# Linformer attention and a squared-ReLU FFN on one core: first stages by head pairs, and pauses on GpSimd between the first load issues

## Chip, cores, metric

One NeuronCore of a Trainium2 chip. The metric is the device time of one execution in microseconds. A "span" is the time from the first to the last instruction of a profiled execution; here it is 1.7 to 2.2 us shorter than the device time.

## The reference

```python
def _attn_ref(q, k, v, E, F):            # q, k, v: (8, 8, 1024, 64), E, F: (64, 1024)
    k_proj = np.einsum('ks,bhsd->bhkd', E, k)
    v_proj = np.einsum('ks,bhsd->bhkd', F, v)
    scores = q @ k_proj^T / sqrt(64); attn = softmax(scores)       # shortened
    return attn @ v_proj
# then x = (8192, 512) and the FFN: relu(x @ w_in)**2 @ w_out, w_in (512, 2048), w_out (2048, 512)
```

## The kernel before

A batch has 8 heads of 1024 rows. The kernel has long been tuned: while the FFN of one batch runs, the attention of the next is fitted between its matmuls. Only batch 0 has nothing to hide behind. Its first half of rows is done in `first_stages`, and the FFN of that half follows at once. All inputs except `E` and `F` come in through GpSimd's queue, which casts fp32 to bf16 on the way. The loads are issued in the order in which they are needed:

```python
    for s in (slice(0, 4), slice(4, 8)):
        load_heads(K_first, k, s)                # two pieces of K, batch 0
    ident = const_pool.tile([P, P], BF16, name="ident")
    make_identity(nc, ident[:])
    load_q_half(0, slice(0, H))                  # the first half of Q's rows
    for s in (slice(0, 4), slice(4, 6), slice(6, 8)):
        load_heads(V_first, v, s)                # three pieces of V
    # ... then w_in in pieces, the second half of Q, w_out; later K, V, Q of batch 1
```

```python
        def first_stages(self):
            # filler(n): n matmuls of 512 columns whose result nobody reads
            filler(2); self.project_k(0); filler(1); self.transpose_k(0)
            self.project_k(1); filler(2); self.transpose_k(1); filler(1)     # (joined lines)
            for g in range(2):
                self.half_transpose_q(0, g, ffn_psum)
            for g in range(2):
                self.half_scores(0, g)
                self.half_exponentials(g)
            heads = [slice(0, 4), slice(4, 6), slice(6, 8)]
            self.project_v(heads[0])
            self.copy_v(heads[0])
            self.half_sums(0, apart=True)
            self.half_sums(1)
            self.half_reciprocals(0)
            self.half_reciprocals(1)
            self.half_values(0)
            for s in heads[1:]:
                self.project_v(s)
                self.copy_v(s)
            self.half_values(1)
            for g in range(2):
                for e in range(2):
                    self.half_normalize(0, g, e)         # writes xT, what the FFN reads
```

The FFN of batch 0 opens with 16 matmuls of 512 columns: four column blocks of `xT`, each against four blocks of `w_in`. At step 33 of the FFN, K and V of batch 1 are projected (`project`, into the tile `ps_kv`). That is the first use of batch 1's loads.

The softmax here doesn't subtract the row's maximum and nothing guards it: scores larger than these inputs give would overflow.

## Time and profile before

| | before |
|---|---|
| time, median of 3 runs (range) | 484.47 us (483.62 to 485.47) |
| span of the profiled run | 482.4 us |
| TensorE busy, share of the span | 97% |
| first FFN matmul starts | 21.05 us |
| V of batch 1 has landed | 53.27 us |
| first matmul on V of batch 1 | 53.32 us |

A landing, here and below, is the last of the 16 DMA engines' completion marks of one load, read from the trace's record. Lines of the page (busy us, share of the span, instructions):

```profile
span 482.4 us, 8423 instructions
...
PE 470.3 (97%) x3630; PEld 292.6 (61%) x3630; DVE 314.1 (65%) x382; ACT 261.5 (54%) x413; POOL 34.7 (7%) x48
...
q0 software_dynamic: 30624, 29.36, 39.4%
...
HBM read 59.24 MB, written 16.78 MB: 158 GB/s over the span
```

TensorE (PE) is all but full, so the kernel as a whole is bound by its matmuls. GpSimd's queue (q0) wrote 29.36 MB for 59.24 MB read: the cast halves the bytes, and a rate of 204 GB/s in the trace stands for 408 GB/s of reads.

The view by stretches, 4 to 12 us: first the stretch, then each engine's busy time, last what the loads wrote in GB/s.

```profile
4.00:6.00 2.00, 0.70 (x8) 0.57 (x8) 0.97 (x2) 0.00 (x0) 2.00 (x4) 1.00 1.10 175
6.00:8.00 2.00, 0.51 (x8) 0.51 (x8) 0.14 (x1) 1.04 (x1) 2.00 (x3) 1.00 1.08 145
8.00:10.00 2.00, 2.00 (x11) 0.96 (x10) 0.00 (x0) 0.59 (x1) 0.71 (x2) 1.00 1.20 191
10.00:12.00 2.00, 1.68 (x10) 0.77 (x8) 0.64 (x2) 0.00 (x0) 0.10 (x1) 1.00 1.38 197
```

From 10 us on the rate stays at 197 to 209 GB/s until 40 us. From 4 to 8 us it is lower, and in that time GpSimd issues loads without a gap.

The timeline before, cut (start, us, engine, line, operation, out<-in, count; in brackets the idle time ahead of it and what ended it):

```profile
3.00 0.90 POOL L97 DMA_DIRECT2D Q_sb<-in_q_dram  x1
...
4.21 2.42 POOL L93 DMA_DIRECT2D V_sb<-in_v_dram  x3
...
6.62 1.40 POOL L124 DMA_DIRECT2D w_in<-in_moe_w_in_dram  x2
...
9.11 1.92 PE L262 MATMUL ps_k<-K_sb,ET 128*64 128x256 bf16 x8
...
12.00 1.06 PE L262 MATMUL ps_k<-K_sb,ET 128*64 128x256 bf16 x8
...
19.43 0.48 PEld L284 LDWEIGHTS <-FT 128*64 128x64 bf16 x16 [0.21 <-DMA V_sb<-in_v_dram]
...
20.11 0.29 DVE L288 CAST vp<-ps_v 128x128 bf16<-128x128 f32 x1 [0.39 <-PE ps_v L284]
...
20.32 2.47 DVE L351 TENSOR_TENSOR xT<-ps_att,rs 128x512 bf16<-128x512 f32 x4
...
21.05 6.40 PE L459 MATMUL ps_h<-xT,w_in 128*128 128x512 bf16 x28 [0.19 <-DVE xT L351]
```

V's last piece lands at 19.39 us; its projection, a copy and one normalization lie between that and the first FFN matmul, 1.67 us in all.

The same view at 53 us, K and V of batch 1:

```profile
53.03 0.40 PE L180 MATMUL ps_kv<-K_sb,ET 128*64 128x512 bf16 x1
53.32 0.38 PE L181 MATMUL ps_kv<-V_sb,FT 128*64 128x512 bf16 x1
```

### The profile page before, as it was taken

The numbers are of one execution on the slowest core, as the hardware profiler recorded it, in microseconds if no ns is written. First come the engines' busy times: TensorE is split into PE (matmuls) and PEld (weight loads), VectorE is DVE, ScalarE is ACT, GpSimd is POOL, SyncE is SP. The second block draws the span as 40 slices with busy tenths as digits, with TensorE's granted clock in tenths as the row PEclk, the third lists the DMA queues.
The fourth block names the chain that finished last, engine by engine and source line by source line (L and its number), as shares of the span: only waits on it lengthen the run. The fifth ranks groups of instructions, "written<-read, shape, count | busy, mean of one in ns | idle before, by whom it ended". The sixth has DMA issues, their size and how long they took to land.

```text
span 482.4 us, 8423 instructions
## 1 busy us (share of the span) xinstructions
PE 470.3 (97%) x3630; PEld 292.6 (61%) x3630; DVE 314.1 (65%) x382; ACT 261.5 (54%) x413; POOL 34.7 (7%) x48
## 2 busy tenths in 40 slices
PE   4899999999999999999999999999999999999997
PEld 2544676475574746657475665747557474666656
DVE  1478955554958559493776848667494855948383
ACT  2387544758427564466635667176662756545351
POOL 6540020020020001000010000100000000000000
PEclk9999999999999999999999999999999999999999
DMA  9999989579989086941859147690702102020202
GB/s 155 203 204 207 168 181 200 137 120 229 180 128 229 12 175 88 180 94 50 153 86 227 22 115 131 91 200 1 165 11 75 25 1 88 1 88 0 88 1 87
DMA packets 72789, 55.46 MB, mean 115 GB/s; under 512 B 33968, under 2 KB 64944, under 8 KB 72752
## 3 DMA queue, kind: packets, MB, share of 16 engines
q0 software_dynamic: 30624, 29.36, 39.4%
q1 hardware_dynamic: 42128, 25.56, 21.1%
q8 instruction: 28, 0.46, 0.4%
q14 instruction: 9, 0.07, 0.0%
HBM read 59.24 MB, written 16.78 MB: 158 GB/s over the span
## 4 chain that ended last, share of the span: by engine, by line
PE 92%; DVE 3%; DMA 3%; ACT 1%; POOL 1%; issue 0%; POOLq 0%
PE ps_h L459 44%; PE ps_y L479 23%; PE ps_z L479 11%; PE ps_x L479 6%; DMA V_sb<-in_v_dram 3%; PE ps_kv L180 2%; PE ps_att L221 2%; PE ps_att L206 2%; DVE hsq L521 1%; DVE s L473 1%; PE ps_v L284 0%; DVE xT L246 0%; DVE xT L351 0%; PE ps_kv L181 0%; ACT h_relu L513 0%; POOL K_sb L93 0%
## 5 line engine op out<-in xcount | busy, mean ns | idle before, releaser
L459 PE MATMUL ps_h<-xT,w_in 128*128 128x512 bf16 x1024 | 224.8, 379 | 0.2 <-DVE xT L351 0.2
L521 DVE TENSOR_TENSOR hsq<-h_relu 128x1024 bf16<-128x1024 f32 x123 | 149.9, 1222 | 75.0 <-ACT h_relu L513 74.2
L513 ACT ACTIVATE h_relu<-ps_h 128x512 f32<-128x512 f32 x255 | 149.4, 597 | 63.4 <-PE ps_h L459 63.0
L459 PEld LDWEIGHTS <-w_in 128*128 128x128 bf16 x1024 | 99.7, 98 | 117.7 <-issue 1.9
L479 PEld LDWEIGHTS <-s 128*128 128x128 bf16 x1024 | 98.5, 98 | 19.8 <-issue 8.7
L479 PEld LDWEIGHTS <-hsq 128*128 128x128 bf16 x768 | 73.8, 98 | 17.3 <-issue 3.8
L479 PE MATMUL ps_y<-T,s 128*128 128x256 bf16 x512 | 62.4, 273 | 0.0
L246 DVE TENSOR_TENSOR xT<-ps_att,rs 128x1024 bf16<-128x1024 f32 x28 | 33.4, 1215 | 17.6 <-ACT rs L236 17.0
L473 DVE TENSOR_TENSOR s<-hsq 128x1024 bf16<-128x1024 bf16 x64 | 43.5, 683 | 0.0
L591 ACT COPY o_sb<-ps_y 128x512 f32<-128x512 f32 x15 | 8.8, 586 | 53.8 <-PE ps_y L479 53.7
L213 ACT ACTIVATE expT<-ps_att 128x1024 bf16<-128x1024 f32 x28 | 27.2, 1025 | 14.0 <-PE ps_att L206 14.0
L479 PE MATMUL ps_x<-w_out,hsq 128*128 128x256 bf16 x256 | 33.2, 273 | 0.0
L479 PE MATMUL ps_y<-w_out,hsq 128*128 128x256 bf16 x256 | 33.2, 273 | 0.0
L595 DVE TENSOR_TENSOR o_sb<-ps_z,p_b 128x512 f32<-128x512 f32 x16 | 11.0, 688 | 33.8 <-issue 19.9
L479 PE MATMUL ps_y<-T,hsq 128*128 128x256 bf16 x256 | 30.9, 272 | 0.0
L479 PE MATMUL ps_z<-T,s 128*128 128x256 bf16 x256 | 30.6, 273 | 0.0
L479 PE MATMUL ps_z<-w_out,s 128*128 128x256 bf16 x256 | 30.6, 273 | 0.0
L591 ACT COPY p_b<-ps_y 128x512 f32<-128x512 f32 (+1 forms) x17 | 9.4, 556 | 25.9 <-PE ps_y L479 25.8
L81 POOL DMA_DIRECT2D Q_sb<-in_q_dram x7 | 6.1, 876 | 227.7 <-DMA qT<-Q_sb 227.2
L473 DVE TENSOR_TENSOR s<-s,hsq 128x1024 bf16<-128x1024 bf16 x32 | 21.8, 684 | 0.3
L473 DVE TENSOR_TENSOR s<-hsq,s 128x1024 bf16<-128x1024 bf16 x32 | 21.7, 682 | 0.0
L591 ACT COPY p_a<-ps_y 128x512 f32<-128x512 f32 (+1 forms) x17 | 9.4, 561 | 21.8 <-PE ps_y L479 21.6
(75 smaller groups left out, 233.0 us busy)
## 6 DMA issues: line engine op xcount, KB each, us to landing
out_dram<-o_sb SPq DMA_DIRECT2D x30, 512.0 KB, 3.8
K_sb<-in_k_dram POOLq DMA_DIRECT2D x7, 1024.0 KB, 15.3
V_sb<-in_v_dram POOLq DMA_DIRECT2D x7, 1024.0 KB, 22.4
Q_sb<-in_q_dram POOLq DMA_DIRECT2D x7, 1024.0 KB, 9.4
w_out<-in_moe_w_out_dram POOLq DMA_DIRECT2D x4, 512.0 KB, 13.2
w_in<-in_moe_w_in_dram POOLq DMA_DIRECT2D x7, 256.0 KB, 10.0
K_sb<-in_k_dram POOLq DMA_DIRECT2D x2, 512.0 KB, 8.5
out_dram<-o_sb SPq DMA_DIRECT2D x3, 256.0 KB, 2.1
```

What stands on the lines that cost most here:

```text
L180: nc.tensor.matmul(ps[0:KP, :], lhsT=ET[:, i, :], rhs=kv[:, :, i, :], start=f, stop=l)
L206: nc.tensor.matmul(ps[o, bank, :], lhsT=self.kT[r, 2 * pr + j, :], start=True, stop=True, rhs=self.qT[r, NT * (2 * pr + j):NT * (2 * pr + ...
L213: nc.scalar.activation(e[:], self.ps["s", pr][:], AF.Exp, scale=SCALE)
L221: nc.tensor.matmul(ps[32 * j:32 * j + 32, a, :], lhsT=weights(o, 4 * g + j), rhs=self.exp[2 * g + j // 2][o, bank, :], start=True, stop=Tr ...
L246: nc.vector.tensor_tensor(out=self.xT[:, 2 * g + e].rearrange("p a n t -> p a (n t)"), in0=self.ps["v", g, e][:], in1=self.rs[g][:], op=AL ...
L459: nc.tensor.matmul(ps[:], lhsT=w_in_blk(cb, fb), rhs=xT[:, cb, :, 2 * ch:2 * ch + 2], start=(cb == 0), stop=(cb == NCB - 1),)
L473: nc.vector.tensor_tensor(out=s[o][:, js], in0=x, in1=y, op=op)
L479: nc.tensor.matmul(ps[tb] if len(ps) == 2 else ps[0][:, tb], lhsT=lhs[:, j, tb * P:(tb + 1) * P], rhs=rhs[:, j], start=first and n == 0 an ...
L513: nc.scalar.activation(r[:, n], ps[:], AF.Relu)
L521: multiply = lambda: nc.vector.tensor_tensor(out=o, in0=r[:], in1=r[:], op=ALU.mult)
L591: nc.scalar.copy(to[:, t], ps)
L595: nc.vector.tensor_tensor(out=to[:, t], in0=ps, in1=more[:, t], op=ALU.add)
```

## The change

The intent: let the FFN start sooner by working in smaller pieces and by moving out of its way what it does not need at once; and space out the issues of the first loads, so that GpSimd is not issuing without a break while K is on its way.

```diff
     make_identity(nc, ident[:])
+    idle = const_pool.tile([P, 1024], BF16, name="idle")
+    def pause(n):
+        for _ in range(n):
+            nc.gpsimd.memset(idle[:], 0.0)
+    pause(1)
     load_q_half(0, slice(0, H))
-    for s in (slice(0, 4), slice(4, 6), slice(6, 8)):
+    for n, s in enumerate((slice(0, 4), slice(4, 6), slice(6, 8))):
+        pause(2 if n == 0 else 1)
         load_heads(V_first, v, s)
 ...                                             # (half_transpose_q now takes any heads and a copy function)
             self.transpose_k(1)
-            filler(1)
-            for g in range(2):
-                self.half_transpose_q(0, g, ffn_psum)
+            for n in range(4):
+                self.half_transpose_q(
+                    0, range(2 * n, 2 * n + 2), ffn_psum, nc.scalar.copy if n == 1 else nc.vector.tensor_copy)
 ...
+            self.half_sums(0, apart=True)
             self.project_v(heads[0])
             self.copy_v(heads[0])
-            self.half_sums(0, apart=True)
 ...
             self.half_values(0)
+            self.half_normalize(0, 0, 0)
             for s in heads[1:]:
                 self.project_v(s)
                 self.copy_v(s)
+            self.half_normalize(0, 0, 1)
+        def last_of_first(self):                 # called after the first four FFN matmuls
             self.half_values(1)
-            for g in range(2):
-                for e in range(2):
-                    self.half_normalize(0, g, e)
+            for e in range(2):
+                self.half_normalize(0, 1, e)
```

The built program spreads the five memsets differently from the source: one ahead of Q, one ahead of each of V's three pieces, one ahead of `w_in`.

## The prediction

> **What bounds the kernel now.** The page: 482.4 us span, PE busy 97%, granted clock 1.00 throughout. From 21.05 us, the first FFN matmul (L459), PE hardly waits again: the waits list for PE after 20 us adds up to 0.4 us. So only the first 21 us, and what ties later PE work to the loads, can give time. 2% (9.7 us) is out of reach.
>
> The loads are a second bound, up to 56 us. The software queue lands 29.36 MB while HBM reads 59.24 MB (fp32 in, bf16 out). In the stretch view it lands 197 to 209 GB/s in every 2 us from 10 to 40 us, about 410 GB/s of reads, without a bubble. (The Trainium skill, "DMA: Bandwidth & Descriptors", "Where 436 GB/s comes from", gives 358 for HBM; the trace shows more.) The exception is 4 to 10 us: 175, 145 and 191 GB/s, while GpSimd issues Q, V and w_in back to back (timeline, 3.0 to 8.0 us). The shortfall to 204 GB/s is (29+59+13) x 2 = about 200 KB, so about 1.0 us of delay, carried by every later load. The last load that matters: V of batch 1 is issued at 30.31 us and lands 23.0 us later (tile view), at 53.3 us; its first projection matmul (L181) starts at 53.32, where PE arrived about 0.1 us before. A PE that is merely earlier waits there.
>
> **What the change does.**
> - Compute order (both builds): Q is transposed and copied in four pieces, one copy on ScalarE; a filler matmul is dropped; row sums go ahead of V's projection; the first normalization goes ahead of V's last two copies; values and normalizations of heads 4-7 go behind the first four FFN matmuls. The last V copy (20.11-20.40) and a normalization (0.61) no longer stand between V's last projection (ends 20.09) and the FFN (21.05): 0.95 us sooner. But 0.4 us of values matmuls falls inside the PE-bound part: 0.5 us net.
> - Pauses: five GpSimd memsets of 128x1024 bf16 (in the build: one ahead of Q, one ahead of each piece of V, one ahead of w_in). The 128x128 memset took 0.23 us and a 128x1 one 0.10, so I estimate 1.1 us each, linearly. Q is then issued near 4.5 us, V near 6.5, 8.6 and 10.4, w_in near 12.2, still ahead of their turn (Q starts to land at about 12, w_in at 19): no bubble. Isolated issues later (0.7 us in every 1.3, 18 to 28 us) go with 198 to 207 GB/s, so I expect most of the dip to go: 0.4 to 1.0 us of earlier landings.
>
> **On the critical path.** Total gain = the smaller of the PE gain (about 0.5 us plus the shift of the loads) and the shift of V of batch 1 at 53 us (plus 0.1). I take 0.9 us: 483.6. Range 482.3 to 484.9. Faster by over 2%: 0.01; within 2%: 0.98; slower: 0.01.
>
> **What would show it.** Landing rates in 4 to 10 us near 200; K, Q and V landing 0.4 to 1.0 us sooner; first FFN matmul at 19.3 to 20.2 us; V of batch 1 landing near 52.5 and the first L181 matmul directly behind it.
>
> **What would make it wrong.** The dip belongs to the start of the loads rather than to back-to-back issues: then landings stay, PE waits for V near 53.3 us, and the gain is about 0.1 us. Memsets over 1.5 us delay the identity (needed at 4.9 us) or starve the queue. The memsets themselves slow the loads.

## The result

| | before | after |
|---|---|---|
| time, median of 6 runs (range) | 484.18 us (483.19 to 485.47) | 484.62 us (484.03 to 485.38) |
| ratio to before, 95% interval | | 1.0008 (0.9989 to 1.0027) |
| span of the profiled run | 482.4 us | 482.9 us |
| V's first piece has landed | 16.78 us | 15.84 us |
| V's last piece has landed | 19.39 us | 18.47 us |
| first FFN matmul | 21.05 us | 21.28 us |
| V of batch 1 has landed | 53.27 us | 52.52 us |
| first matmul on V of batch 1 | 53.32 us | 53.80 us |

A ratio is the mean time of one kernel's fast runs over that of the other's of the same rounds, so not quite the ratio of the medians. The time is the same within noise. Yet this pair of profiles looked odd: the first pieces of K, Q and V landed 0.6 to 1.0 us earlier and V of batch 1 0.75 us earlier, and TensorE was later all the same.

Lines of the page after:

```profile
span 482.9 us, 8429 instructions
...
PE 471.4 (98%) x3629; PEld 293.0 (61%) x3629; DVE 314.9 (65%) x383; ACT 262.0 (54%) x414; POOL 39.4 (8%) x53
```

The view by stretches after:

```profile
4.00:6.00 2.00, 0.29 (x5) 0.30 (x6) 1.09 (x1) 0.12 (x1) 2.00 (x3) 1.00 1.11 170
6.00:8.00 2.00, 1.43 (x16) 0.99 (x15) 0.42 (x1) 1.21 (x2) 2.00 (x3) 1.00 1.17 187
8.00:10.00 2.00, 2.00 (x9) 1.21 (x8) 0.00 (x0) 0.31 (x1) 2.00 (x4) 1.00 1.24 205
```

The rate from 6 to 10 us is higher than before, as predicted. The timeline after, cut at the same places:

```profile
5.13 1.41 POOL L108 MEMSET idle<- 128x1024 bf16 x1
...
7.23 0.97 POOL L108 MEMSET idle<- 128x1024 bf16 x1
...
8.58 1.92 PE L271 MATMUL ps_k<-K_sb,ET 128*64 128x256 bf16 x8
...
11.86 1.91 PE L271 MATMUL ps_k<-K_sb,ET 128*64 128x256 bf16 x8
...
18.10 0.30 PE L329 MATMUL ps_r<-expT,ones 64*32 64x256 bf16 x8 [0.73 <-ACT expT L323]
...
18.34 1.06 PE L293 MATMUL ps_v<-V_sb,FT 128*64 128x256 bf16 x16
...
20.26 1.08 PE L293 MATMUL ps_v<-V_sb,FT 128*64 128x128 bf16 x32
...
21.28 1.04 PE L473 MATMUL ps_h<-xT,w_in 128*128 128x512 bf16 x4
...
22.25 0.41 PE L329 MATMUL ps_att<-expT,vp 64*32 64x256 bf16 x16
...
22.59 5.63 PE L473 MATMUL ps_h<-xT,w_in 128*128 128x512 bf16 x24
```

Two things stand out. The second projection of K took 1.91 us where before it took 1.06: TensorE's clock had not yet risen. The trace's record of the clock at full begins at 11.2 us before and at 15.9 us after. (The stretch view prints 1.00 for earlier stretches too, because the record has nothing for them; the durations of equal matmuls are what to read.) And V's first projection, whose data had landed at 15.84 us, waits behind the row sums for the exponentials until 18.34.

At 53 us after:

```profile
53.80 0.40 PE L189 MATMUL ps_kv<-K_sb,ET 128*64 128x512 bf16 x1
53.80 0.40 PE L190 MATMUL ps_kv<-V_sb,FT 128*64 128x512 bf16 x1
```

V of batch 1 had landed 1.28 us before that. Here TensorE is the late one.

So I had a theory and rivals. Theory A: the pauses bring the loads forward, and a late rise of the clock ate the gain. Rival B: the new order is worse by itself. Rival C: the earlier landings are chance. Rival D: V of batch 1 is no bound.

### The profile page after: what moved, and what is told of

Read it like the earlier page. It is cut to its first block, busy times and chain, and to the rows that moved or that the text cites. A ratio compares the mean times of both kernels' runs of the same rounds, so it can differ in the third digit from the quotient of the medians.

```text
span 482.9 us, 8429 instructions
## 1 busy us (share of the span) xinstructions
PE 471.4 (98%) x3629; PEld 293.0 (61%) x3629; DVE 314.9 (65%) x383; ACT 262.0 (54%) x414; POOL 39.4 (8%) x53
## 3 DMA queue, kind: packets, MB, share of 16 engines
HBM read 59.24 MB, written 16.78 MB: 157 GB/s over the span
## 4 chain that ended last, share of the span: by engine, by line
PE 94%; DVE 3%; ACT 1%; DMA 1%; issue 0%; SPq 0%
PE ps_h L473 44%; PE ps_y L493 23%; PE ps_z L493 11%; PE ps_x L493 6%; PE ps_kv L189 3%; PE ps_att L230 2%; PE ps_att L215 2%; DVE hsq L535 1%; DMA e_f<-in_F_dram 1%; PE ps_k L271 1%; DVE s L487 1%; DVE xT L255 0%; PE ps_v L293 0%; PE ps_fill L370 0%; ACT h_relu L527 0%; PE ps_q L305 0%
```

## The experiments

### Four kernels with a warmed TensorE

To take the clock out of the comparison, 14 matmuls on a constant tile went in ahead of the first loads, to before, to before plus the pauses alone, to the change without its pauses, and to the whole change. All four ran on one chip beside nine runs of before (median 484.14 us).

```diff
+    warm = const_pool.tile([P, 512], BF16, name="warm")
+    nc.vector.memset(warm[:], 1.0)
     def E_and_F():
+        warm_up(10)                  # matmuls with lhsT=warm[:, 0:P], rhs=warm[:]
         for t, src, copy in (...):
             ...
             copy(t[:], ps[:])
+            if t is ET:
+                warm_up(4)
```

Expected of before, warmed:

> The kernel before, with 14 matmuls on a constant tile ahead of the first loads, so that TensorE is busy from about 1.3 us. Theory A (the clock of TensorE rises only after a stretch of steady work, and in the profile of after it rose 4.6 us later than in that of before, which ate the earlier loads): granted clock full by about 8 us, first FFN matmul at 20.8 to 21.1 us (bound by V's landing at 19.4), V of batch 1 lands near 53.3 us and its first matmul starts just behind; time 0 to 0.5 us under before. Rival B (the clock is no matter, the order of the changed first stages is worse by itself): same time as before within 0.3 us, and the same place of the first FFN matmul.

Expected of before with the pauses alone, warmed:

> Before plus the pauses alone, plus the same 14 warming matmuls. Theory A: K, Q and V land 0.6 to 1.0 us earlier than in before_warm, V of batch 1 near 52.5 us, the first FFN matmul about 20.2 us; time 0.7 to 0.9 us under before_warm. Rival B: the time is that of before_warm, as nothing of the order changed. Rival C (the earlier landings in the profile of after are chance, not the pauses): landings as in before_warm within 0.2 us, V of batch 1 near 53.3 us, no gain.

Expected of the change without its pauses, warmed:

> After without the pauses, plus the same 14 warming matmuls. Theory A: first FFN matmul near 20.1 us, about 0.9 us sooner than in before_warm, but V of batch 1 still lands near 53.3 us and TensorE waits for it there 0.3 to 0.7 us: time within 0.2 us of before_warm. Rival B: 0.4 us or more over before_warm. Rival D (V of batch 1 is no bound): 0.4 to 0.5 us under before_warm.

Expected of the whole change, warmed:

> The whole change plus the same 14 warming matmuls. Theory A: full clock by 8 us, V of batch 1 near 52.5 us with TensorE waiting for it there; first FFN matmul 19.2 to 19.7 us; time 0.7 to 0.9 us under before_warm, as pauses_warm. Rival B: no faster than before_warm. Rival D: about 1.2 us under before_warm, pauses and order adding up.

Measured (landings and starts in us):

| | before_warm | pauses_warm | reorder_warm | after_warm |
|---|---|---|---|---|
| clock at full from | 6.0 | 4.4 | 7.1 | 6.1 |
| V's first piece landed | 15.64 | 16.17 | 15.41 | 15.89 |
| V's last piece landed | 18.27 | 18.85 | 18.09 | 18.58 |
| second piece of `w_in` landed | 20.83 | 20.09 | 20.60 | 21.11 |
| first FFN matmul | 19.94 | 20.52 | 20.38 | 19.70 |
| 16th FFN matmul | 23.69 | 23.75 | 24.15 | 24.50 |
| time, median | 483.81 | 483.90 | 484.33 | 483.68 |
| ratio to before | 0.9989 (0.9976 to 1.0003) | 0.9994 (0.9981 to 1.0006) | 1.0005 (0.9992 to 1.0017) | 0.9993 (0.9980 to 1.0005) |

None of the four differs from before beyond noise. With and without pauses, the medians of the two pairs differ with opposite signs: pauses_warm is 0.09 us over before_warm, after_warm 0.65 us under reorder_warm. (Inside the span before_warm is shorter: its five runs have spans of 481.5 to 482.0 us, the nine of before 482.0 to 483.3. A third of the 0.8 us between the means is lost again outside the span, 2.02 against 1.77 us. Whether the early clock or earlier loads did this, the record does not tell.) What the traces say is clearer. The clock did rise early, as expected. But before_warm has no pauses and lands V sooner than pauses_warm. Its stretches, then those of pauses_warm:

```profile
4.00:6.00 2.00, 2.00 (x7) 0.58 (x6) 0.90 (x1) 0.00 (x0) 2.00 (x4) 1.00 1.16 189
6.00:8.00 2.00, 2.00 (x20) 1.30 (x20) 0.43 (x1) 1.05 (x1) 1.76 (x3) 1.00 1.23 201
```

```profile
4.00:6.00 2.00, 1.55 (x10) 0.64 (x9) 1.18 (x1) 0.00 (x0) 2.00 (x3) 1.00 1.17 184
6.00:8.00 2.00, 2.00 (x20) 1.26 (x19) 0.42 (x1) 1.04 (x1) 2.00 (x3) 1.00 1.20 170
```

GpSimd issues as closely in before_warm as in before (its busy time from 6 to 8 us is 1.76 of 2.00), and there is no dip: 201 GB/s. That contradicts theory A as far as the pauses go, and supports rival C. In both kernels with the new order the 16th FFN matmul came later than in their partners (by 0.46 and 0.75 us), which speaks for B, but late pieces of `w_in` are mixed in (in before_warm too). In reorder_warm even the first FFN matmul waited for it:

```profile
20.38 1.04 PE L483 MATMUL ps_h<-xT,w_in 128*128 128x512 bf16 x4 [1.41 <-DMA w_in<-in_moe_w_in_dram]
```

### The two kernels again, unchanged

If the landings and the clock are chance, repeats of one kernel must scatter. No edit; three single looks, and one look at the change with timed rounds (11 runs of before on this chip, median 483.84 us).

> The kernel before, unchanged, to see how much one profile differs from another. In its first profile the clock of TensorE was full from 11.2 us, the loads landed 175 and 145 GB/s in 4 to 6 and 6 to 8 us, and the first piece of V landed at 16.8 us. Chance theory (clock rise and early landing rate differ from run to run of one kernel): at least one of the four repeats has its clock rise over 1 us away from the first profile of its kernel, and at least one of the two of before lands over 185 GB/s in 6 to 8 us and V's first piece before 16.2 us. Systematic rival (back-to-back issues make the dip): both repeats of before dip to 140 to 165 GB/s in 6 to 8 us and land V at 16.6 to 17.0 us.

> The kernel before, unchanged, a second look with the same expectations as the first: the chance theory has another rise of the clock and another landing rate in 6 to 8 us than the first profile, the systematic rival has 140 to 165 GB/s and V's first piece at 16.6 to 17.0 us again.

> The changed kernel, unchanged. In its first profile the clock was full from 15.9 us, V's first piece landed at 15.8 us, the 128th FFN matmul started at 52.6 us. Chance theory: the clock rises at another time (any of 9 to 16 us) and where it rises before 12.5 us the first FFN matmul comes at 19.7 to 20.6 us and the first projection matmul of batch 1 at 53.0 to 53.4 us. Systematic rival (pauses and the dropped filler always cost one more window): it rises at 15 to 16.5 us again. Timed: within 0.2% of before in both theories, more likely above than below.

> The changed kernel, unchanged, a second look with the same expectations as the first: chance theory, a clock rise over 1 us away from 15.9 us in one of the two and the rest following from it; systematic rival, 15 to 16.5 us again.

| | before | before_again1 | before_again2 | after | after_again1 | after_again2 |
|---|---|---|---|---|---|---|
| clock at full from | 11.2 | 13.7 | 11.3 | 15.9 | 11.0 | 13.7 |
| GB/s in 6 to 8 us | 145 | 157 | 167 | 187 | 170 | 193 |
| V's first piece landed | 16.78 | 16.95 | 15.97 | 15.84 | 15.84 | 16.41 |
| V's last piece landed | 19.39 | 19.58 | 18.60 | 18.47 | 18.47 | 19.10 |
| first FFN matmul | 21.05 | 21.69 | 20.27 | 21.28 | 19.69 | 20.74 |
| 16th FFN matmul | 24.29 | 24.92 | 23.56 | 25.06 | 23.73 | 24.51 |
| V of batch 1 landed | 53.27 | 53.89 | 52.61 | 52.52 | 52.52 | 52.46 |
| first matmul on it | 53.32 | 53.93 | 52.65 | 53.80 | 52.56 | 53.26 |
| span | 482.4 | 483.0 | 481.7 | 482.9 | 481.6 | 482.4 |

Timed again, the change is at 484.29 us, ratio 1.0005 (0.9990 to 1.0021).

The clock rises at different times in one and the same kernel, near 11, 13.7 and 15.9 us: the systematic rival, a late rise in every run of the changed kernel, falls. Whether the change makes a late rise more likely, three profiles of each kernel cannot tell; it drops one filler, and putting that one back was not tried. My chance theory also asked that one repeat of before land over 185 GB/s from 6 to 8 us; neither did (157 and 167), so that expectation was missed, and before_again1 (157 GB/s, V at 16.95 us) lies inside the figures of the rival that blames the issues. But V's first piece lands at 15.97 us in before_again2, almost as early as in the earliest profile with pauses (15.84). Missed too: in after_again1 the first projection matmul of batch 1 came at 52.47 us, not at 53.0 to 53.4.

In after_again1 the clock was early. There the change shows at its best, and the loads are the limit at 53 us again:

```profile
16.52 0.30 PE L329 MATMUL ps_r<-expT,ones 64*32 64x256 bf16 x8 [0.73 <-ACT expT L323]
16.75 1.06 PE L293 MATMUL ps_v<-V_sb,FT 128*64 128x256 bf16 x16
...
19.69 1.04 PE L473 MATMUL ps_h<-xT,w_in 128*128 128x512 bf16 x4
```

```profile
52.47 0.40 PE L189 MATMUL ps_kv<-K_sb,ET 128*64 128x512 bf16 x1
52.56 0.38 PE L190 MATMUL ps_kv<-V_sb,FT 128*64 128x512 bf16 x1
```

The first FFN matmul comes 1.22 us after V's last piece, where before needs 1.67 at an early clock: 0.45 us sooner, not the 0.95 that I had predicted. V's first piece lay in place from 15.84 us and was projected only at 16.75, since the row sums stand ahead of it.

### V's projection back ahead of the sums, with and without pauses

These two, the next and the last ran on one chip beside 11 runs of before (median 484.31 us).

```diff
-            self.half_sums(0, apart=True)
             self.project_v(heads[0])
             self.copy_v(heads[0])
+            self.half_sums(0, apart=True)
```

> The changed kernel with V's first projection put back ahead of the first row sums. In a repeat of the changed kernel TensorE idled 0.7 us for the first exponentials while V's first piece lay landed, and the first FFN matmul came 1.2 us after V's last piece, not the 0.7 I had reckoned. Theory E (the order of sums and projection serializes TensorE): with the clock full by 12.5 us, first FFN matmul 0.75 to 0.95 us after V's last piece and the 16th 4.6 to 4.85 us after it (changed kernel 5.0 to 5.4, before 4.90); a late clock or a late first piece of w_in adds to it. Rival (the softmax chain on ScalarE decides): still 1.1 to 1.3 and 5.0 to 5.4 us. Time in both within 0.15% of before.

The second also drops the memsets (`pass` in their place).

> As v_first without the five pauses. If the pauses do nothing for the landings (as ten profiles so far say): V's first piece lands anywhere in 15.4 to 17.0 us, landing rate in 4 to 8 us 145 to 205 GB/s, time within 0.1% of v_first. If the pauses help by more than chance: V's first piece at 16.5 to 17.0 us and 0.1 to 0.2% slower than v_first. No memset takes turns with VectorE, so the copies of kp take 0.42 and 0.22 us.

| | v_first | v_first_no_pauses |
|---|---|---|
| clock at full from | 13.9 | 13.4 |
| GB/s in 4 to 6 and 6 to 8 us | 172, 165 | 176, 167 |
| V's first, last piece landed | 17.00, 19.56 | 16.62, 19.26 |
| first FFN matmul after V's last piece | 1.26 us | 0.95 us |
| 16th after V's last piece | 5.02 us | 4.82 us |
| time, median; ratio to before | 484.73; 1.0011 (0.9996 to 1.0027) | 484.35; 1.0003 (0.9987 to 1.0020) |

The clock rose late in both. Without pauses, V's projection no longer waits and the lag is 0.95 us, within theory E:

```profile
16.67 1.06 PE L293 MATMUL ps_v<-V_sb,FT 128*64 128x256 bf16 x16
...
17.66 0.30 PE L329 MATMUL ps_r<-expT,ones 64*32 64x256 bf16 x8
...
20.20 1.02 PE L473 MATMUL ps_h<-xT,w_in 128*128 128x512 bf16 x4 [0.27 <-DVE xT L360]
```

With pauses it is 1.26 us, within the rival's figures. In both, the first normalization then waited for ScalarE's reciprocals (1.38 us in v_first, 1.26 without pauses), here in v_first:

```profile
20.08 0.69 DVE L360 TENSOR_TENSOR xT<-ps_att,rs 128x512 bf16<-128x512 f32 x1 [1.38 <-ACT rs L351]
```

Against after_again2, whose clock was equally late (1.64 us and 5.41 us), both are better. So the order of sums and projection costs 0.4 to 0.7 us of lag in these single profiles (1.64 - 1.26 and 1.64 - 0.95), and once it is mended the softmax chain on ScalarE is next. The split of the two is not settled by one profile each. And the pauses: same rates, same landings within what chance does, same time within noise (medians 484.73 with them, 484.35 without).

### The last values ahead of the FFN again

```diff
             self.half_normalize(0, 0, 1)
-        def last_of_first(self):
             self.half_values(1)
 ...
-        1: "last_of_first", 7: "second_half 0 0", ...
+        7: "second_half 0 0", ...
```

> The changed kernel with the values and normalizations of heads 4 to 7 put back ahead of the FFN. Theory: moving them behind the first four FFN matmuls only shifts them; from the first to the 16th FFN matmul it is now 3.24 us (before) and not 3.77, the first FFN matmul comes 0.4 to 0.6 us later relative to V's last piece (1.6 to 1.8 us), and the 16th stands at 4.9 to 5.1 us after V's last piece: the time does not change by more than 0.1% against the changed kernel. Rival (the move is what costs the 0.5 us seen in both pairs of warmed kernels): 16th at 4.4 to 4.7 us.

The clock was at full from 10.8 us. From the first to the 16th FFN matmul it took 3.27 us (the change: 3.77 to 4.04 in its three profiles):

```profile
20.01 1.96 DVE L360 TENSOR_TENSOR xT<-ps_att,rs 128x512 bf16<-128x512 f32 x3
...
20.48 4.71 PE L471 MATMUL ps_h<-xT,w_in 128*128 128x512 bf16 x20
```

The first FFN matmul came 1.92 us after V's last piece and the 16th 5.19 us after it; in after_again1 the 16th stood at 5.26 us. So the move shifts work and gains nothing: what it takes out ahead of the FFN it puts back inside. I was 0.1 us off in both lags. Time 483.83 us, ratio 0.9996 (0.9975 to 1.0018).

### No fillers

Is the clock's rise of any weight for the time? The change with its filler matmuls taken out:

```diff
             def filler(n):
+                return
                 ps = ffn_psum("ps_fill")
```

> The changed kernel with its five filler matmuls taken out, so that TensorE is less steadily busy before the scores. Clock theory: the clock rises at 14 us or later, mostly at 16 to 21 us, the 16th FFN matmul stands 6 us or more after V's last piece, and the time is 0.5 to 2 us (0.1 to 0.4%) over that of before. Rival (the clock rise does not matter for the time): same time as the changed kernel, 16th at 5.0 to 5.4 us.

The clock rose at 23.4 us only. The second projection of K at 13.10 and V's first projection at 20.03 still run at half speed:

```profile
13.10 1.91 PE L271 MATMUL ps_k<-K_sb,ET 128*64 128x256 bf16 x8
...
20.03 1.92 PE L293 MATMUL ps_v<-V_sb,FT 128*64 128x256 bf16 x16
...
24.22 1.04 PE L474 MATMUL ps_h<-xT,w_in 128*128 128x512 bf16 x4
```

The first FFN matmul came 3.91 us after V's last piece, the 16th 7.69 us. The time is 487.96 us, ratio 1.0074 (1.0059 to 1.0090): the only difference that is clear of noise, and larger than I had expected. Part of the delay in this one profile (about 1 us) is a late landing of V's last piece, 20.31 us.

### What the fourteen profiles say together

In all fourteen the span is the start of the first matmul on V of batch 1 plus 429.06 to 429.11 us (before: 482.4 - 53.32; after: 482.9 - 53.80; no_fillers: 485.8 - 56.74). All that differs between their spans is decided by then. That matmul starts 0.04 us after V's landing in six of them (before and its two repeats, after_again1, v_first_no_pauses, last_back): the loads decide. In pauses_warm it is 0.05 us, directly behind the matmul on K: a tie. In the others TensorE comes 0.09 to 3.16 us after the landing: TensorE decides. Where V has long landed, its first matmul starts 0.003 us after that on K; in the six it starts 0.06 to 0.29 us after it. So the two bounds lie within 0.3 us of each other there, and an earlier landing of V of batch 1 alone could have gained no more than that.

No effect of the pauses on the landings shows. V's first piece: mean 16.23 us over the six profiles without pauses (15.41 to 16.95), 16.35 over the eight with them (15.84 to 17.69). V of batch 1: 52.89 without, 52.78 with, and 52.3 to 53.9 over all. These means mix kernels, warmed and not, and chips; with such scatter they could hide an effect of some tenths of a us.

The marks of the single DMA engines tell where the scatter comes from. K's first piece is issued at 1.25 us, before any pause (the first pause, at 3.0 us, falls into its transfer). Its first engine is done at 7.16 to 7.45 us in all fourteen profiles, its last at 7.67 to 9.95 us (mean 8.42 without pauses, 8.48 with). From there on pauses make no difference: V's first piece lands 7.74 to 8.05 us after K's first piece in every profile, with pauses and without. So most of what looked like an effect of the pauses is a lag of some engines that is there by 10 us at the latest. Why they lag more in one run than in another stays open.

Of the rivals: C is borne out. D falls for the runs in which the loads decide. B is not settled: at an early clock the 16th FFN matmul stands 5.26 us after V's last piece in after_again1, 4.90 and 4.96 in two profiles of before, and no timed pair is clear of noise. The dropped filler and the four-piece transposes of Q were not tested alone.

## Why the prediction was right or wrong

- **The range and "within 2%" were right, the range by luck.** The 2% (9.7 us) were safe: the largest effect of any edit here, no_fillers, was 3.65 us. The range from 482.3 to 484.9 us held because it also contains no change at all; both steps that made up the gain failed.
- **The point was off in sign.** I took 0.9 us of gain; the two timed comparisons say 1.0008 and 1.0005, that is 0.2 to 0.4 us slower, not clear of noise. Inside the span the kernels are level: the mean is 482.5 and 482.2 us in the two timed groups of after, 482.4 to 482.5 in three groups of before. The rest is the 0.35 us more that kernels with the new order spend outside the span (2.11 to 2.13 against 1.76 us), on which the prediction has nothing. The first FFN matmul came in the forecast place, 19.3 to 20.2 us, in one of three profiles (19.69, 20.74, 21.28).
- **"So I expect most of the dip to go" failed.** I read one profile's low rate from 4 to 8 us as the effect of back-to-back issues, because the two coincided. before_warm and reorder_warm issue back to back and land 201 and 205 GB/s from 6 to 8 us; kernels with pauses land 165 to 193. The first pair of profiles agreed with me by chance, as far as the repeats tell, down to the 0.7 us at 53 us. The prediction itself named what comes nearest, that the dip belongs to the start of the loads: the lag is there in K's first piece. What makes it differ from run to run stays open.
- **"No longer stand between ... 0.95 us sooner" was mis-sized.** At an early clock it is 0.45 us (1.67 to 1.22 us after V's last piece, after_again1). I had taken out the copy and the normalization but not seen that the sums, now first, hold V's projection until the exponentials are done. Mending that gave 0.95 us of lag in one profile (predicted: 1.67 - 0.95 = 0.72). `w_in` limits it too, which I left out of the text: its second piece lands 1.2 to 1.4 us after V's last piece in eleven of the fourteen profiles and 2.5 in the other three, so the third FFN matmul cannot start before that.
- **"0.4 us of values matmuls falls inside" was 0.54 us** (3.77 against 3.23 us from the first to the 16th FFN matmul). Put together from two profiles of the change, the sum is 1.22 + 3.77 = 4.99 against 1.67 + 3.23 = 4.90 us; in after_again1 itself, where a piece of `w_in` was late as well, it is 1.22 + 4.04 = 5.26. The predicted 0.5 us net is nothing, or a small loss. last_back shows the same from the other side.
- **"A PE that is merely earlier waits there" was right.** In six of fourteen profiles TensorE waits for V of batch 1, in a seventh it comes just as V lands. There a gain in the order alone could not have shown. The wait in the profile before was 0.29 us, not "about 0.1".
- **TensorE's clock was taken as constant.** "Granted clock 1.00 throughout" came from views that print 1.00 where the record has nothing. The Trainium skill, "TensorE: Matmul & The Clock Gate", Part 1, says that the clock starts at half and is released by sustained activity, seen through a free-running window of about 3.4 us, and that this varies from run to run. The traces agree: eight equal matmuls take 1.92 and 1.06 us, and the rise came at 11.0, 13.7 and 15.9 us in three runs of one kernel. In the profile of after TensorE was 1.28 us behind the loads; in after_again1, the same kernel with an early clock, it waited for them. I had seen the fillers in the code and two durations of one matmul group in the trace, and asked neither why.
- **Memsets and issue times were nearly right:** 0.97 to 0.99 us each (1.41 for the one beside VectorE's cast) against my 1.1; Q issued at 4.23, V at 6.49, 8.13 and 9.71, `w_in` at 11.30 us (I had 4.5, 6.5, 8.6, 10.4 and 12.2), and no bubble.

## What to carry to other kernels

When two bounds run side by side, first find the one event through which both must pass, and measure its slack: here the span was that event's start plus a constant, so a gain ahead of it that did not move it was worth nothing. Check too that the time outside the span is the same in both kernels. Before a dip in one profile is explained, look at a second profile of the same kernel; a coincidence in time with a busy engine is not a cause. And a stretch of idle matmuls in a tuned kernel may be its most valuable part: taking out five fillers cost 0.74%, four times what I had hoped to gain from the whole change.

## What the Trainium skill lacked or had wrong

- "TensorE: Matmul & The Clock Gate", Part 1, advises against fitting to the number of slow matmuls, as the ramp is under 1% of a kernel. In this kernel the ramp at its worst (no fillers) cost 0.74%, and between runs of one unchanged kernel the rise moved from 11.0 to 15.9 us. In the three profiles of after the span went with the rise (481.6, 482.4 and 482.9 us), in those of before, where the loads decide, it did not. The page does not say what a tuner of 0.1% steps sees of this.
- "DMA: Bandwidth & Descriptors" gives a fixed and a per-byte cost for one load. Here the 16 engines finished one and the same load 0.4 to 2.5 us apart (K's first piece: 0.4 us in reorder_warm, 1.6 in before, 2.5 in no_fillers), differently from run to run of one kernel. The page says that two engines are usually slower ("Latency and other measured facts"), but gives no size for such a scatter, and a load is only as early as its last engine. The 358 GB/s that the prediction took from this page are a core's half of an HBM stack; under "Bandwidth" the page measures up to 425 GB/s for a core whose neighbour is idle, so the reads of about 410 GB/s here (204 GB/s landed in bf16) do not show it wrong.
- "GPSIMD Engine Reference", § 1 Specifications, says that GpSimd shares its SBUF interfaces with VectorE, with contention for some VectorE instructions. The traces agree: in all eight profiles with pauses the memset beside VectorE's cast of E took 1.41 us and the next two 0.97 to 0.98. It works the other way too: in five of them VectorE's copy of `kp` ran beside the fifth memset, which ended at 11.40 us; whether it had begun at 10.00 or at 11.03, the copy ended at 11.5 and so took 0.45 to 1.48 us, against 0.22 in before. That section gives no size for this; other pages of the skill say more, so this is a number for this kernel and no gap.
- "Runtime: NRT & Kernel Launch", Terms, says that instruction memory is refilled in 16 KiB blocks. The trace shows such packets of 16 KB and about 0.9 us while the loads run (at 20.55 us before, 18.72 in before_warm). In the four warmed kernels the first load to finish after the packet's end had 1.6 to 2.1 us between its first and last engine, the load ahead of it 0.5 to 0.9; in before it was 1.4 ahead of the packet and 1.5 after it. No page says what such a packet costs a load beside it; no run here tested it by itself.
